# Two pieces of work for the output projection move from its first steps into the last unit of attention

## The chip, the cores and the metric

The kernel runs on one core of a Trainium2 chip. A core has five engines, each with its own instruction queue that is worked off strictly in order: PE (TensorE, matrix products), DVE (VectorE), ACT (ScalarE), POOL (GpSimd) and SP (SyncE, here only a queue that issues transfers). Engines wait for each other through semaphores. The metric is the time of one execution on the device in microseconds; lower is better. All times below are in microseconds unless ns stands there.

## What is computed

```
xn = layernorm(x)                                   # 2048 tokens, 448 features
q, k, v = xn @ wq, xn @ wk, xn @ wv                 # 16 heads of 28, 4 blocks of 512 tokens
for each block s:
    a_dot = softmax(causal(q_s k_s^T)) v_s          # local attention
    a_mem = phi(q_s) M / (phi(q_s) z + 1e-6)        # memory of the blocks before
    o_s   = g * a_mem + (1 - g) * a_dot ;  M, z += phi(k_s)^T v_s, sum phi(k_s)
out = x + o @ wo + (sigmoid(xn @ w_gate) * (xn @ w_up)) @ w_down
```

All data are 32-bit floats. Products go through PE in a 32-bit format that keeps fewer bits, so both factors are split into a high part and a low remainder, and a product of 448 terms becomes eleven matrix instructions (high by high, high by low, low by high, for three chunks of 128 features and one of 64; in the code this list is `TERMS`).

## The kernel before

The kernel has a front part, in which x is normalised and transposed into four tiles `xs[0..3]` (one for each block of 512 tokens: 128 partitions, chunks 0 to 3 the high part, 4 to 6 the low one), and q, k, v are made and stored. Then one long part is written out by hand, and that is where the change is. It weaves three streams, each a Python generator that issues instructions up to its next `yield`:

- `gated()`, the feed-forward branch: `pgu` products (L254) of `xs` with the gate and up weights, `sg` (tanh on ACT, L261; product on DVE, L271), `hh` split into high (ACT, L277) and low (DVE, L280), and the `pd` products (L180) that DVE adds to `acc` (L182). It works on two columns of 128 hidden features at a time, and for these on the blocks 0 to 3. The six last groups of `pd` are left over (`rest`): two for block 2, then four for block 3.
- `attention()`, sixteen units of four heads, each unit two pairs of heads. A table of ticks sets the order: a unit has 28 ticks, and `at(tick, rank, work)` puts a step in a tick's list, where lower ranks come first. A pair has scores (`st`, L638), maxima, a subtraction in three parts (DVE, L702) and exponentials in three parts (ACT, L706); the next unit's ticks hold the unit's end: `finish`, the product `pa` (L724) of the exponentials `w` with the values, and then `back`, `divide`, `turn`, `store`, which transpose the result on DVE (L730, L736), divide it, and add it to the memory part in DRAM (`od`, a transfer from POOL's queue).
- `project()`, the output projection. For each tile of 128 tokens (four to a block) there is a split, `split_tokens(b, t)`: ACT copies the high part of the attention result `sums` into `xs` (L802), and DVE subtracts it to get the low part (two instructions, L109 and L110). Two steps after a tile's split comes its product `po` of eleven instructions (L820) with the output weights `wo`. DVE adds it to `acc` (L827), and the tile is stored (L829). One of the groups in `rest` follows each of the first six `po`.

`sums[b]` is read back from `od[b]` by eight transfers of SP's queue (`load_sums`, L796); for block 0 the first is given out after the last scores of the last pair but one. The `xs` tile of a block is used again for `sums`, since the feed-forward branch has read it for the last time by then. The two halves of `wo` are split by ACT (L92) and DVE (L93) during the last hidden features.

The tile scheduler is switched off in this part. The order in each engine's queue is the order in which the Python code calls the instructions, and only the semaphores are added. A main loop at the end takes a step of `gated()` or `project()` in turn and lets `attention()` catch up to its share.

Of the kernel before, what the change touches and what calls it, by code (L numbers as in the profile page):

```python
# [11 lines left out]
AF = mybir.ActivationFunctionType  # L12
# [4 lines left out]
P = 128  # L17
# [21 lines left out]
TICKS = 28  # L39
# [3 lines left out]
SUBTRACT = ((22, 25, 26), (33, 34, 37))  # L43
EXPONENTS = ((25, 27, 31), (34, 36, 39))
BEHIND = (17, 18, 19, 24)
SUMS, END = 15, 25


# [20 lines left out]
def kernel(  # L69
# [11 lines left out]
    V, A, G, T = nc.vector, nc.scalar, nc.gpsimd, nc.tensor  # L81
# [6 lines left out]
    xs = [keep.tile([P, 7, L], F32R, name=f"xs{b}") for b in range(NB)]  # L88
# [18 lines left out]
    def transpose_low(p3, dst, t):  # L107
        tok = slice(t * P, (t + 1) * P)
        V.tensor_sub(dst[:, 4:7, tok], p3[:, 0:3], dst[:, 0:3, tok].bitcast(F32))  # L109
        V.tensor_sub(dst[64:, 3, tok], p3[64:, 3], dst[64:, 3, tok].bitcast(F32))  # L110
# [11 lines left out]
    def bank(name, tag):  # L122
        return ps.tile([P, L], F32, name=name, tag=tag, bufs=banks[tag])
# [177 lines left out]
    with tc.tile_pool(name="front", bufs=2) as sb, tc.manual_schedule(engines=FRONT):  # L301
# [227 lines left out]
        for b in range(NB):  # L529
# [24 lines left out]
            for k, c in enumerate((3, 4, 5, 6, 0, 1, 2) if last else range(7)):  # L554
# [34 lines left out]
                n = k - 1 if b == 0 else k + 1  # L589
# [152 lines left out]
    pairs = [Pair(n) for n in range(NB * H // 2)]  # L742
    units = [Unit(u, pairs[2 * u:2 * u + 2]) for u in range(NB * NG)]

    def attention():
        for n in range(2):
            pairs[n].load()
        units[0].load_values()
        yield
        plan = [[] for _ in range(n_att + 1)]  # L750

        def at(tick, rank, work, *args):
            plan[tick].append((rank, work, args))

        def following(n):
            if n < len(pairs):
                pairs[n].load()
            else:
                load_sums(n - len(pairs))

        for n, pair in enumerate(pairs):
            first = TICKS * (n // 2)
            ticks = [first + tick for tick in SCORES[n % 2]]
            for k, tick in enumerate(ticks):
                at(tick, 0, pair.score, k)
            at(ticks[-1], 2, following, n + 2)
            for k in range(3):
                at(first + MAXIMA[n % 2][k], 3, pair.maximum, k + 2)
                at(first + SUBTRACT[n % 2][k], 5, pair.subtract, k)
                at(first + EXPONENTS[n % 2][k], 1, pair.exponents, k)  # L770
            for k in range(4):
                at(first + JOINS[n % 2][k], 4, pair.join, k)
        for u, unit in enumerate(units):
            first = TICKS * (u + 1)
            at(first + SUMS, 1, unit.finish)
            if u + 1 < len(units):
                at(first + SUMS, 2, units[u + 1].load_values)
            for tick, work in zip(BEHIND, (unit.back, unit.divide, unit.turn, unit.store)):
                at(first + tick, 6, work)
        for work in plan:  # L780
            for _, run, args in sorted(work, key=lambda w: w[0]):
                run(*args)
            yield

    sums = {}

    def load_sums(b):

        if b < 2:
            sums[b] = sb.tile([P, HG, L], F32, name="sums", tag="qk2", bufs=2)  # L790
        else:
            sums[b] = sums[b - 2]
        o3 = od[b].rearrange("(h c) n -> h c n", c=32)
        for m in range(8):
            a, c = m % 2, 4 * min(m, 6)
            nc.sync.dma_start(sums[b][64 * a:64 * a + 64, m // 2, :], o3[:, c:c + 4, :])  # L796

    def project():

        def split_tokens(b, t):  # L800
            o3 = sums[b][:, :, t * P:(t + 1) * P]
            A.activation(xs[b][:, 0:4, t * P:(t + 1) * P], o3, AF.Copy)  # L802
            transpose_low(o3, xs[b], t)

        def out_weights(w):
            at = 2 * D * (w // 4) + D * (w % 2)
            return wo[w % 4 // 2][:, at:at + D]

        yield
        for n in range(NB * NT + 2):  # L810
            if n < NB * NT:
                b, t = divmod(n, NT)
                split_tokens(b, t)
                if t == NT - 1 and b + 2 < NB:
                    load_sums(b + 2)
            if n >= 2:
                b, t = divmod(n - 2, NT)
                po = bank("po", ("p", "gu")[n % 2])
                for m, (a, w) in enumerate(TERMS):
                    T.matmul(po[:, :D], xs[b][:, a, t * P:(t + 1) * P], out_weights(w),  # L820
                             start=m == 0, stop=m == len(TERMS) - 1)
                    if m in (3, 7):
                        yield
                halves = 2 if n == NB * NT + 1 else 1
                for i in range(halves):
                    part = slice(D // halves * i, D // halves * (i + 1))
                    V.tensor_add(acc[b][:, t, part], po[:, part], acc[b][:, t, part])  # L827
                    queue = nc.scalar if i else nc.sync
                    queue.dma_start(out[b * L + t * P:b * L + (t + 1) * P, part], acc[b][:, t, part])  # L829
                yield  # L830
                if rest:
                    yield from rest.pop(0)

    N_OUT = 1 + NB * NT * 3 + 12
    steps = attention()
    n_att = len(units) * TICKS + END
    done = 0
    with tc.manual_schedule(engines=MANUAL):
        next(steps)
        k = sum(FILLS) + 6  # L840
        for part in (ffn, project()):
            for _ in part:
                want = min(round(n_att * (k - LEAD) / (N_FFN + N_OUT - LEAD - TAIL)), n_att)
                k += 1
                while done < want:
                    next(steps)
                    done += 1
# [39 lines left out]
```

## Time and profile before

| | |
|---|---|
| median of 3 runs | 687.49 (686.54 to 687.96) |
| the profiled execution's own time | 686.53 |
| its span, first to last instruction | 684.8 |
| granted TensorE clock | 1.000 |
| PE busy | 678.9 |
| DVE busy | 570.8 |
| ACT busy | 338.6 |
| POOL busy | 141.6 |

The profile is of one execution. A line that names an engine, a source line and an operation gives the tiles as "written <- read", then shapes, and "x11" for eleven instructions in a row. PEld is the loading of weights into PE, beside PE itself. "SPq" and "ACTq" are an engine's queue at work on something that isn't counted as busy, such as a wait or a transfer that is issued. A bracket such as [0.67 <-DVE xs L109] says that the engine stood idle for 0.67 us before this work, and that DVE's work on `xs` in line 109 ended the wait. PE's instructions overlap: the duration of one is its way through the array, and the distance from start to start is what it costs in a stream.

### The profile page before, as it was taken

The numbers are of one execution on the slowest core, as the hardware profiler recorded it, in microseconds if no ns is written. First come the engines' busy times: TensorE is split into PE (matmuls) and PEld (weight loads), VectorE is DVE, ScalarE is ACT, GpSimd is POOL, SyncE is SP. The second block draws the span as 40 slices with busy tenths as digits, with TensorE's granted clock in tenths as the row PEclk, the third lists the DMA queues.
The fourth block names the chain that finished last, engine by engine and source line by source line (L and its number), as shares of the span: only waits on it lengthen the run. The fifth ranks groups of instructions, "written<-read, shape, count | busy, mean of one in ns | idle before, by whom it ended". The sixth has DMA issues, their size and how long they took to land.

```text
span 684.8 us, 10503 instructions
## 1 busy us (share of the span) xinstructions
PE 678.9 (99%) x3594; PEld 567.8 (83%) x3594; DVE 570.8 (83%) x995; ACT 338.6 (49%) x563; POOL 141.6 (21%) x349
## 2 busy tenths in 40 slices
PE   8999999999999999999999999999999999999998
PEld 7898878778878788887888878888787887888797
DVE  6765695766799899999999899899998998999754
ACT  5837555343364445645456455455544554544320
POOL 3500010101212232232212213132122231321000
PEclk9999999999999999999999999999999999999999
DMA  7446556696224331252324442324352332423352
GB/s 268 182 151 234 203 208 243 245 335 184 71 73 99 95 100 58 58 154 61 96 56 101 96 113 60 100 57 105 85 111 69 97 74 72 106 71 85 82 168 104
DMA packets 45940, 84.37 MB, mean 123 GB/s; under 512 B 6336, under 2 KB 20544, under 8 KB 45376
## 3 DMA queue, kind: packets, MB, share of 16 engines
q1 hardware_dynamic: 42736, 76.26, 37.0%
q0 software_dynamic: 3008, 7.34, 5.0%
q8 instruction: 28, 0.46, 0.3%
q14 instruction: 24, 0.20, 0.1%
q10 hardware_dynamic: 144, 0.11, 0.0%
HBM read 51.05 MB, written 32.64 MB: 122 GB/s over the span
## 4 chain that ended last, share of the span: by engine, by line
PE 89%; DVE 7%; issue 2%; POOL 1%; ACT 1%; DMA 0%; DVEq 0%; ACTq 0%; POOLq 0%
PE pgu L254 37%; PE pd L180 18%; PE pp L380 10%; PE st L638 5%; PE po L820 5%; PE pa L724 5%; PE pv L360 5%; PE pmm L408 2%; PE n L426 2%; DVE w L702 1%; DVE mx L660 1%; PE pt L102 1%; PE pk L400 1%; DVE acc L182 1%; DVE sg L271 0%
## 5 line engine op out<-in xcount | busy, mean ns | idle before, releaser
L254 PE MATMUL pgu<-xs,wgu 128*128 128x512 f32 x1232 | 302.6, 393 | 0.0
L254 PEld LDWEIGHTS pgu<-xs,wgu 128*128 128x128 f32 x1232 | 229.1, 188 | 46.2 <-issue 2.0
L180 PE MATMUL pd<-wdn,hh 128*128 128x448 f32 x672 | 155.3, 366 | 0.0
L180 PEld LDWEIGHTS pd<-wdn,hh 128*128 128x128 f32 x672 | 122.8, 188 | 11.5 <-issue 0.8
L653 POOL TENSOR_SCALAR_AFFINE_SELECT w<-w 128x256 f32<-128x256 f32 (+1 forms) x160 | 76.0, 478 | 231.2 <-ACT w L642 162.8
L706 ACT ACTIVATE w<-w 128x1024 f32<-128x1024 f32 (+1 forms) x96 | 87.9, 916 | 58.0 <-DVE w L702 58.0
L642 ACT ACTIVATE w<-st 128x512 f32<-128x512 f32 x128 | 75.7, 592 | 61.5 <-PE st L638 55.9
L702 DVE TENSOR_TENSOR w<-w,mb 128x1024 f32<-128x1024 f32 (+1 forms) x96 | 100.7, 1055 | 0.8
L660 DVE TRANSPOSE_TENSOR_REDUCE mx<-w 128x32 f32<-128x1024 f32 x64 | 79.0, 1234 | 6.6 <-POOL w L653 6.5
L380 PE MATMUL pp<-xs,wqk 128*128 128x512 f32 x308 | 77.7, 402 | 0.0
L182 DVE TENSOR_TENSOR acc<-pd,acc 128x448 f32<-128x448 f32 x112 | 67.6, 603 | 5.5 <-PE pd L180 5.5
L277 ACT ACTIVATE hh<-sg 128x512 fp32r<-128x512 f32 x56 | 35.4, 631 | 67.3 <-DVE sg L271 45.6
L380 PEld LDWEIGHTS pp<-xs,wqk 128*128 128x128 f32 x308 | 56.8, 188 | 13.4 <-issue 2.4
L638 PE MATMUL st<-qk 84*128 84x128 f32 (+3 forms) x256 | 62.0, 314 | 0.0
L261 ACT ACTIVATE sg<-pgu 128x512 f32<-128x512 f32 x56 | 33.2, 593 | 50.7 <-PE pgu L254 48.8
L638 PEld LDWEIGHTS st<-qk 84*128 84x128 f32 x256 | 47.9, 189 | 8.7 <-issue 1.4
L271 DVE SCALAR_TENSOR_TENSOR sg<-sg,pgu 128x512 f32<-128x512 f32 x56 | 37.8, 674 | 10.8 <-PE pgu L254 10.8
L387 DVE TENSOR_TENSOR qk<-pp,qk 128x512 fp32r<-128x512 f32 x28 | 19.3, 689 | 29.8 <-ACT e L385 23.7
L688 DVE STREAM_TRANSPOSE mb<-top 128x1024 f32<-128x1024 f32 x32 | 39.5, 1235 | 3.3 <-POOL top L685 3.2
L360 PE MATMUL pv<-wv,xs 128*128 128x448 f32 x176 | 39.6, 376 | 0.3 <-POOL wv L457 0.2
L280 DVE SCALAR_TENSOR_TENSOR hh<-sg,hh 128x512 fp32r<-128x512 f32 x56 | 38.2, 682 | 0.9 <-ACT hh L277 0.9
L724 PE MATMUL pa<-w,vv 128*32 128x128 f32 (+3 forms) x512 | 37.8, 436 | 0.0
(100 smaller groups left out, 638.5 us busy)
## 6 DMA issues: line engine op xcount, KB each, us to landing
qk<-qd SPq DMA_DIRECT2D x192, 112.0 KB
qd<-qk SPq DMA_DIRECT2D x28, 512.0 KB
raw<-in_w_ffn SPq DMA_DIRECT2D x14, 512.0 KB
vd<-vst SPq DMA_DIRECT2D x4, 1024.0 KB
vv<-vd SPq DMA_DIRECT2D x16, 256.0 KB
od<-w POOLq DMA_DIRECT2D x16, 256.0 KB, 4.2
sums<-od SPq DMA_DIRECT2D x32, 128.0 KB
out<-acc SPq DMA_DIRECT2D x15, 224.0 KB
```

Of the source, the lines that this page charges most:

```text
L180: T.matmul(pd[:, :D], l, r, start=n == 0, stop=n == len(mms) - 1)
L182: V.tensor_add(acc[b][:, t, :], pd[:, :D], acc[b][:, t, :])
L254: T.matmul(dst, wgu[f][:, w, side * P:(side + 1) * P], xs[b][:, a, :], start=n == 0, stop=n == len(TERMS) - 1)
L360: T.matmul(pv[:, :D], xs[b][:, a, t * P:(t + 1) * P], wv[w], start=n == 0, stop=n == len(TERMS) - 1)
L380: T.matmul(pp, wqk[c][:, w, :], xs[b][:, a, :], start=n == 0, stop=n == len(TERMS) - 1)
L638: T.matmul(st[:, at:at + L - kb * P], self.qk[:KS, 1, h, kb * P:(kb + 1) * P], self.qk[:KS, 0, h, kb * P:], start=True, stop=True)
L642: A.activation(w, st, AF.Copy)
L653: G.affine_select(d, d, pattern=pattern, base=0, channel_multiplier=-1, compare_op=ALU.is_ge, fill=MASK)
L660: V.tensor_reduce(self.mx[:, 32 * h:32 * h + 32], w3[:, h, :2 * L].rearrange("p (b n) -> p b n", n=32), axis=mybir.AxisListType.X, op=ALU. ...
L702: V.tensor_sub(w, w, m)
L706: A.activation(w, w, AF.Exp, scale=SCALE)
L724: T.matmul(pa[32 * j:32 * j + 32, kb * P:], self.vv[:, kb, 32 * j:32 * j + 32], self.pairs[j // 2].block(j % 2, kb), start=kb == 0, stop=k ...
```

## The change

The splits of the first two tiles (block 0, tiles 0 and 1) are given out at ticks 10 and 12 of the last unit's trailing ticks, with the highest rank, 7, so as the last thing in their tick. They fall out of the projection's loop, which begins its splits with the third tile. `split_tokens` moves up so that both streams can call it. With that, all line numbers rise, by 1 up to line 745 and by 4 to 8 below; the copy of the high part becomes L748, and DVE's two instructions become L110 and L111.

```diff
+EARLY_SPLITS = (10, 12)
 ...
+    def split_tokens(b, t):
+        o3 = sums[b][:, :, t * P:(t + 1) * P]
+        A.activation(xs[b][:, 0:4, t * P:(t + 1) * P], o3, AF.Copy)
+        transpose_low(o3, xs[b], t)
+
     def attention():
 ...
             for tick, work in zip(BEHIND, (unit.back, unit.divide, unit.turn, unit.store)):
                 at(first + tick, 6, work)
+        for t in range(2):
+            at(TICKS * len(units) + EARLY_SPLITS[t], 7, split_tokens, 0, t)
 ...
     def project():
-        def split_tokens(b, t):
 ...
                 b, t = divmod(n, NT)
-                split_tokens(b, t)
+                if n > 1:
+                    split_tokens(b, t)
```

On DVE, at the seam between attention and projection, the rows before are these. `xs_65` is the tile of block 0, `acc_71` the sum of block 2, and L730 is `back` of the last unit. The last two rows are the split of tile 0, and the same two stand behind them for tile 1 and for tile 2.

```order
L702 TENSOR_TENSOR w<-w,mb 128x2x2x128
L182 TENSOR_TENSOR acc_71<-pd,acc_71 128x448
L93 TENSOR_TENSOR wo<-raw,wo 128x896
L271 SCALAR_TENSOR_TENSOR sg<-sg,pgu 128x512
L182 TENSOR_TENSOR acc_71<-pd,acc_71 128x448
L280 SCALAR_TENSOR_TENSOR hh<-sg,hh 128x512
L730 STREAM_TRANSPOSE w<-pa 128x512
L109 TENSOR_TENSOR xs_65<-sums,xs_65 128x3x128
L110 TENSOR_TENSOR xs_65<-sums,xs_65 64x128
```

And on DVE now:

```order
L703 TENSOR_TENSOR w<-w,mb 128x2x2x128
L110 TENSOR_TENSOR xs_65<-sums,xs_65 128x3x128
L111 TENSOR_TENSOR xs_65<-sums,xs_65 64x128
L183 TENSOR_TENSOR acc_71<-pd,acc_71 128x448
L110 TENSOR_TENSOR xs_65<-sums,xs_65 128x3x128
L111 TENSOR_TENSOR xs_65<-sums,xs_65 64x128
L94 TENSOR_TENSOR wo<-raw,wo 128x896
L272 SCALAR_TENSOR_TENSOR sg<-sg,pgu 128x512
L183 TENSOR_TENSOR acc_71<-pd,acc_71 128x448
L281 SCALAR_TENSOR_TENSOR hh<-sg,hh 128x512
L731 STREAM_TRANSPOSE w<-pa 128x512
```

The pairs of tile 0 and tile 1 moved up, past `wo`, `sg`, `hh`, `back` and two additions to `acc`; the pair of tile 2 now stands right behind `back`.

On ACT, at the same seam, with the semaphores that each row waits for, before:

```order
L706 ACTIVATE w<-w 128x2x2x256 [waits DVE_49,Activation_49,Pool_49]
L706 ACTIVATE w<-w 128x2x2x128 [waits DVE_49,Pool_49]
L92 ACTIVATE wo<-raw 128x896 [waits DMAHW7_49]
L277 ACTIVATE hh<-sg 128x512 [waits DVE_49]
L802 ACTIVATE xs_65<-sums 128x4x128 [waits DMAHW4_49,DMAHW5_49,DMAHW3_49,DMAHW6_49,DMAHW2_49,DMAHW7_49,DMAHW1_49,DMAHW0_49]
L802 ACTIVATE xs_65<-sums 128x4x128 x3
```

And on ACT now:

```order
L707 ACTIVATE w<-w 128x2x2x256 [waits DVE_49,Activation_49,Pool_49]
L748 ACTIVATE xs_65<-sums 128x4x128 [waits DMAHW4_49,DMAHW5_49,DMAHW3_49,DMAHW6_49,DMAHW2_49,DMAHW7_49,DMAHW1_49,DMAHW0_49]
L707 ACTIVATE w<-w 128x2x2x128 [waits DVE_49,Pool_49]
L748 ACTIVATE xs_65<-sums 128x4x128
L93 ACTIVATE wo<-raw 128x896
L278 ACTIVATE hh<-sg 128x512 [waits DVE_49]
L748 ACTIVATE xs_65<-sums 128x4x128 x2
```

The first copy, with its wait for the eight transfers of `sums`, moved ahead of the last exponentials of attention, and the second stands right behind them. On PE, POOL and SP the order of the instructions is the same as before; what PE waits for changes.

More of the change, by code (lines that the diff above doesn't have):

```diff
@@ L798, in project @@
     def project():
-        def split_tokens(b, t):
-            o3 = sums[b][:, :, t * P:(t + 1) * P]
-            A.activation(xs[b][:, 0:4, t * P:(t + 1) * P], o3, AF.Copy)
-            transpose_low(o3, xs[b], t)
         def out_weights(w):
```

## The prediction

> **What bounds the kernel now.** I read the page's first part first: who is busy.
>
> ```profile
> span 684.8 us, 10503 instructions
> PE 678.9 (99%) x3594; PEld 567.8 (83%) x3594; DVE 570.8 (83%) x995; ACT 338.6 (49%) x563; POOL 141.6 (21%) x349
> PEclk9999999999999999999999999999999999999999
> ```
>
> PE is busy 678.9 of 684.8 us at the full granted clock. An edit that leaves PE's work as it is can only win PE's idle time, 5.9 us in all, and only the part of it that the moved work causes. So the next view is PE's waits from 600 us on (total, times, longest), and after it PE's instructions in order of time around the seam between attention and projection (start, duration, what, and in brackets the idle time before it).
>
> ```profile
> PE po L820 <- DVE xs L109: 0.7, 1, 0.7
> ```
>
> ```profile
> 634.19 1.38 PE L180 MATMUL pd<-wdn,hh 128*128 128x448 f32 x6
> 635.50 2.36 PE L724 MATMUL pa<-w,vv 128*32 128x512 f32 x32
> 637.79 0.68 PE L820 MATMUL po<-wo,xs 128*128 128x448 f32 x2
> 639.13 2.08 PE L820 MATMUL po<-wo,xs 128*128 128x448 f32 x9 [0.67 <-DVE xs L109]
> 641.05 1.36 PE L180 MATMUL pd<-wdn,hh 128*128 128x448 f32 x6
> 642.25 2.36 PE L820 MATMUL po<-wo,xs 128*128 128x448 f32 x11
> 644.45 1.36 PE L180 MATMUL pd<-wdn,hh 128*128 128x448 f32 x6
> ...
> 647.85 1.36 PE L180 MATMUL pd<-wdn,hh 128*128 128x448 f32 x6
> ...
> 659.25 22.16 PE L820 MATMUL po<-wo,xs 128*128 128x448 f32 x110
> ```
>
> In these last 85 us PE waits once. The first product of the projection starts when `pa` is done. Its first two instructions run, the third needs the low part of `xs`, and DVE hasn't written that yet. After 639.13 PE has no gap up to its last matrix instruction, so whatever is won at this place reaches the end, and nothing more can be won there. Behind PE's end stand only the last addition and the last transfer, which the change doesn't touch.
>
> Why is DVE late? Its own instructions in order of time:
>
> ```profile
> 632.32 0.69 DVE L702 TENSOR_TENSOR w<-w,mb 128x512 f32<-128x512 f32 x1
> 632.92 0.62 DVE L182 TENSOR_TENSOR acc<-pd,acc 128x448 f32<-128x448 f32 x1
> 634.60 1.09 DVE L93 TENSOR_TENSOR wo<-raw,wo 128x896 fp32r<-128x896 f32 x1 [1.06 <-ACT wo L92]
> 635.61 0.68 DVE L271 SCALAR_TENSOR_TENSOR sg<-sg,pgu 128x512 f32<-128x512 f32 x1
> 636.21 0.62 DVE L182 TENSOR_TENSOR acc<-pd,acc 128x448 f32<-128x448 f32 x1
> 636.99 0.69 DVE L280 SCALAR_TENSOR_TENSOR hh<-sg,hh 128x512 fp32r<-128x512 f32 x1 [0.16 <-ACT hh L277]
> 637.92 0.72 DVE L730 STREAM_TRANSPOSE w<-pa 128x512 f32<-128x512 f32 x1 [0.24 <-PE pa L724]
> 638.57 0.52 DVE L109 TENSOR_TENSOR xs<-sums,xs 128x384 fp32r<-128x384 f32 x1
> 639.11 0.29 DVE L110 TENSOR_TENSOR xs<-sums,xs 64x128 fp32r<-64x128 f32 x1
> 639.43 0.56 DVE L109 TENSOR_TENSOR xs<-sums,xs 128x384 fp32r<-128x384 f32 x1
> ```
>
> The split that PE needs (638.57) stands in the queue behind `back` (637.92), which itself has to wait for the end of `pa`. So the split can't begin before PE is through with `pa`, and PE wants it 0.4 us later. Meanwhile DVE was idle for 1.06 us at 633.5.
>
> **The removed wait.** The row says 0.67 us of idle, but in a stream PE pays from start to start. The disturbed product takes 641.05 - 637.79 = 3.26 us up to the next group, the next one 644.45 - 642.25 = 2.20 us. The wait therefore costs 3.26 - 2.20 = 1.06 us. The two ends are 0.67 (the idle row alone) and 1.06; I take 1.06, because it compares two starts of the same eleven instructions, and the instruction's way through the array stands in the idle row's place on both sides. A page of the Trainium skill puts the undisturbed product lower: "TensorE: Matmul & The Clock Gate", section "Back-to-back issue gap", gives a lone stream N/2.4 + 2.5 ns, for N = 448 some 189 ns, while the trace has 2.20 / 11 = 200 ns; by the page eleven would take 2.08 us and the gain would be 1.18 us, by the row 1.06, and the row decides.
>
> **What moves on ACT.** ACT's instructions in order of time, the copies' durations (least, median, most), and the chain of waits where the copies begin:
>
> ```profile
> 631.67 1.06 ACT L706 ACTIVATE w<-w 128x1024 f32<-128x1024 f32 x1
> 633.10 0.64 ACT L706 ACTIVATE w<-w 128x512 f32<-128x512 f32 x1 [0.37 <-DVE w L702]
> 633.64 0.94 ACT L92 ACTIVATE wo<-raw 128x896 fp32r<-128x896 f32 x1
> 636.33 0.63 ACT L277 ACTIVATE hh<-sg 128x512 fp32r<-128x512 f32 x1 [1.76 <-DVE sg L271]
> 636.87 4.26 ACT L802 ACTIVATE xs<-sums 128x512 fp32r<-128x512 f32 x8
> ```
>
> ```profile
> L802 ACT ACTIVATE xs<-sums x16: 612/614/633, 636.9 to 666.1; 128x512 fp32r<-128x512 f32 x16
> ```
>
> ```profile
> 636.39 0.04 ACTq L802
> ...
> 636.95 0.04 ACTq L802
> ```
>
> A copy takes 0.61 us, and in a row one starts every (4.26 - 0.61) / 7 = 0.52 us. The first now stands between the exponentials of 631.67 and of 633.10. It can start at about 632.65 and ends at 633.27. The last exponentials waited until 633.10 for DVE anyway, so they move by about 0.1 us, to 633.2, and end at 633.8. The copy also brings its wait for eight transfers to this place, and behind it stand those exponentials. If the transfers have landed, it is only the queue's steps: before, they ran from 636.39 to 636.95, beside the running `hh` copy (636.33 to 636.96), so they cost nothing, and now they run beside exponentials of 1.06 us. The upper bound, if nothing hid them, is 636.95 - 636.39 = 0.56 us more. PE enters `pa`, which needs these exponentials, at 635.50, 1.76 us after their old end of 633.74, so 0.1 and 0.66 both vanish. Have the transfers landed? SP's queue issued them from 608.28, and the DMA share (second last figure) falls to zero long before 632.6:
>
> ```profile
> 608.28 5.73 SPq L796 DMA_DIRECT2D sums<-od  x8
> ```
>
> ```profile
> 616.00:617.00 1.00, 1.00 (x6) 0.86 (x5) 1.00 (x2) 0.37 (x1) 0.82 (x2) 1.00 0.63 186
> 617.00:618.00 1.00, 1.00 (x6) 0.83 (x5) 1.00 (x3) 0.00 (x0) 0.00 (x0) 1.00 0.00 1
> ```
>
> That leaves some 15 us of slack. The second copy takes 633.7 to 634.35, and the copy of `wo` moves from 633.64 to about 634.3, ending at 635.2 in place of 634.58. On the path: 0.
>
> **What moves on DVE.** A split pair costs 639.43 - 638.57 = 0.86 us, two 1.72. The first starts with ACT's copy, at about 633.3, and ends at 634.15. The addition to `acc` (0.5 to the next start) follows, then the second pair from 634.65 to 635.5, and `wo` from 635.5 to 636.6 in place of 634.60 to 635.69. So 1.06 us of the 1.72 fall into the idle time that stood there, and what follows moves by about 0.9 us. Who waits for that?
> - PE's eighth `po` instruction is the first that needs the low part of the second half of `wo`: 637.79 + 7 x 0.20 = 639.2, against 636.6. Slack 2.6 us.
> - `sg` goes from 635.61 to about 636.5, and so ACT's `hh` to 637.2 and DVE's low `hh` to about 638.6 in place of 637.68. Only block 3's `pd` reads them, and its first group is the one at 647.85, the third of the six left over. Slack over 8 us.
> - The second addition to block 2's `acc` ends at about 637.7 in place of 636.83 and frees a PSUM bank that PE next wants for the group at 644.45, 1.06 us earlier now. Slack over 5 us.
> - `back` goes from 637.92 to about 638.5. But the two pairs behind it are gone, so the third tile's split starts at about 639.2 (before: after 640.3), while its product starts at about 644.6 (before 645.65). `divide`, `turn` and the store of the last unit come about 1 us earlier too.
>
> On the path: 0. SP's, POOL's and PE's queues keep their order, and no transfer is added. What hides the moved work is DVE's idle 1.06 us and the slack before `pa`; were that cover gone, each microsecond by which the last exponentials end after `pa` has come to them would be one on PE. What is late next in place of the removed wait: nothing within 2.6 us.
>
> **Sum.** 684.8 - 1.06 = 683.7 us of span. The profiled execution took 686.53, that is 1.73 around the span, and would take 685.5; the median of the runs, 687.49, lies 0.96 above it, so the forecast in its terms is 686.4 us, 0.15% less.
>
> **Rivals.**
> 1. *The wait stays under another name, wholly or in part.* The place is the same product, and the row that could take over is the split of `wo` on DVE, which is now behind both pairs. For it: everything moved stands ahead of it. Against: 2.6 us of slack. From an end past 639.2 on each microsecond is lost, and at 640.3 the gain is gone: 687.5 us. If only the idle row's 0.67 is won, 686.8. A change that does nothing, since the wait for the low part would only be seen as something else's, would end here too.
> 2. *Slower, by ACT's queue.* The wait for the transfers now stands ahead of the last exponentials. If the first copy could start only where it did before, at 636.87, for a reason that the rows don't show, the exponentials would run from 637.4 to 638.05, and PE, which needs them from the second batch of `pa`'s weights on (635.95, below), would lose 2.1 us in `pa`. Less the 1.06 that are won, that is 1.0 us more: 688.5. It decides from a copy that starts past 634.8 (635.95 less 0.52 and 0.64), and the loss outweighs the gain past 635.9. Against: the DMA share is zero from 617 on.
>
> ```profile
> 635.95 0.13 PEld L724 LDWEIGHTS pa<-w,vv 128*32 128x32 f32 x4 [0.30 <-issue]
> ```
>
> **How the numbers follow.** The forecast has 0.78, rival 1 0.14 and rival 2 0.08. About 0.2% (1.4 us) is what a measurement of this kernel can tell from no change: the runs before span 1.42 us themselves. The forecast's 686.4 lies on the near side of the bound at 686.1; with a scatter of some half a microsecond a good third of its chance falls beyond it, 0.30. Rival 1 is within the bound. Rival 2 reaches it on the slow side in two of three cases, 0.05. That gives faster 0.30, same 0.65, slower 0.05. The range: the lowest run less the whole gain, 686.54 - 1.06 = 685.5, and the highest run with no gain, 687.96; I take 685.4 to 688.0.
>
> **What would show it.** In the changed kernel's trace PE should go from `pa` through eleven `po` without a bracket, the next `pd` 2.2 us after the first `po`, near 640.0; DVE's split pairs should stand near 633.3 and 634.7, ahead of `wo`, and its idle 1.06 us should shrink to a few tenths; ACT's last exponentials should end before 634; PE's only waits left should be those of the start. The prediction is wrong if `pa` starts later than 635.5 or shows a bracket, or if a `po` waits for `wo`, or if the trace is as forecast and the span isn't shorter.

## The result, and the profile after

| | before | after |
|---|---|---|
| median of 18 runs each | 686.98 | 685.74 |
| lowest to highest | 686.53 to 687.96 | 685.43 to 687.24 |
| ratio, 95% interval | 1 | 0.9983 (0.9976 to 0.9990) |
| span of the profiled execution | 684.8 | 684.2 |

The changed kernel is faster by 1.24 us, or 0.18%; the interval reaches from 0.7 to 1.6 us. The forecast was 686.4 within 685.4 to 688.0.

The page's head and PE's waits over the whole execution (total, times, longest) of the changed kernel:

```profile
span 684.2 us, 10501 instructions
PE 678.0 (99%) x3594; PEld 566.7 (83%) x3594; DVE 570.1 (83%) x995; ACT 338.5 (49%) x563; POOL 141.6 (21%) x349
```

```profile
PE warm L468 <- POOL ident masks.py:199: 1.5, 1, 1.5
PE pt L103 <- DVE xn L346: 0.7, 1, 0.7
PE pv L361 <- DVE xs L110: 0.3, 1, 0.3
```

The wait of `po` is gone. All three waits that are left belong to the first 12 us. PE at the seam, in order of time:

```profile
635.82 2.36 PE L725 MATMUL pa<-w,vv 128*32 128x512 f32 x32
638.11 2.48 PE L824 MATMUL po<-wo,xs 128*128 128x448 f32 x11
640.42 1.36 PE L181 MATMUL pd<-wdn,hh 128*128 128x448 f32 x6
641.62 2.36 PE L824 MATMUL po<-wo,xs 128*128 128x448 f32 x11
643.82 1.36 PE L181 MATMUL pd<-wdn,hh 128*128 128x448 f32 x6
```

The eleven instructions of the first product now stand in one row, and the next group starts 640.42 - 638.11 = 2.31 us after them, where it was 3.26. So the seam gave 0.95 us. The second product takes 2.20, as before. DVE and ACT there:

```profile
632.64 0.68 DVE L703 TENSOR_TENSOR w<-w,mb 128x512 f32<-128x512 f32 x1
633.59 0.56 DVE L110 TENSOR_TENSOR xs<-sums,xs 128x384 fp32r<-128x384 f32 x1 [0.27 <-ACT xs L748]
634.18 0.29 DVE L111 TENSOR_TENSOR xs<-sums,xs 64x128 fp32r<-64x128 f32 x1
634.48 0.62 DVE L183 TENSOR_TENSOR acc<-pd,acc 128x448 f32<-128x448 f32 x1
635.02 0.55 DVE L110 TENSOR_TENSOR xs<-sums,xs 128x384 fp32r<-128x384 f32 x1
635.59 0.29 DVE L111 TENSOR_TENSOR xs<-sums,xs 64x128 fp32r<-64x128 f32 x1
635.91 1.09 DVE L94 TENSOR_TENSOR wo<-raw,wo 128x896 fp32r<-128x896 f32 x1
...
638.90 0.71 DVE L731 STREAM_TRANSPOSE w<-pa 128x512 f32<-128x512 f32 x1
```

```profile
631.99 1.05 ACT L707 ACTIVATE w<-w 128x1024 f32<-128x1024 f32 x1
632.94 0.62 ACT L748 ACTIVATE xs<-sums 128x512 fp32r<-128x512 f32 x1
633.46 0.62 ACT L707 ACTIVATE w<-w 128x512 f32<-128x512 f32 x1
633.98 0.61 ACT L748 ACTIVATE xs<-sums 128x512 fp32r<-128x512 f32 x1
```

DVE's idle time of 1.06 us ahead of `wo` has become 0.27 us ahead of the first split. On ACT the first copy starts 0.95 us after the exponentials ahead of it, one instruction's distance: the eight waits for the transfers are not to be seen. The last exponentials end at 634.08, 1.74 us ahead of `pa`.

The spans differ by 0.6 us and not by 0.95, since `pa` starts 0.32 us later than before. That has nothing to do with the seam. In the front part, which is the same in both kernels, PE came to the first product with `wqk` later by 0.42 us (before, then after):

```profile
19.70 7.69 PE L380 MATMUL pp<-xs,wqk 128*128 128x512 f32 x33
```

```profile
20.12 7.64 PE L381 MATMUL pp<-xs,wqk 128*128 128x512 f32 x33
```

By the last `pgu` ahead of the seam it has become 632.00 - 631.67 = 0.33 us, and from there to `pa` it is 3.82 us where it was 3.83: nothing of the shift arises at the seam. From the start of `pa` to the end of the span it is 684.8 - 635.50 = 49.3 us before and 684.2 - 635.82 = 48.4 after.

### The profile page after: what moved, and what is told of

Read it like the earlier page. It is cut to its first block, busy times and chain, and to the rows that moved or that the text cites. A ratio compares the mean times of both kernels' runs of the same rounds, so it can differ in the third digit from the quotient of the medians.

```text
span 684.2 us, 10501 instructions
## 1 busy us (share of the span) xinstructions
PE 678.0 (99%) x3594; PEld 566.7 (83%) x3594; DVE 570.1 (83%) x995; ACT 338.5 (49%) x563; POOL 141.6 (21%) x349
## 4 chain that ended last, share of the span: by engine, by line
PE 97%; DMA 1%; DVE 1%; SPq 0%; ACT 0%; issue 0%; DVEq 0%
PE pgu L255 41%; PE pd L181 20%; PE pp L381 10%; PE st L639 6%; PE pa L725 5%; PE po L824 5%; PE pv L361 5%; PE pmm L409 2%; PE n L427 2%; DMA acc<-in_x 1%; PE pt L103 1%; PE pk L401 1%; DVE stats L320 0%; DVE xs L110 0%; DVE xn L346 0%
## 5 line engine op out<-in xcount | busy, mean ns | idle before, releaser
L262 ACT ACTIVATE sg<-pgu 128x512 f32<-128x512 f32 x56 | 33.2, 592 | 50.8 <-PE pgu L255 48.9
```

## Experiments

The theory is that of the prediction: PE waited for the low part of tile 0 alone, and this was late because in DVE's queue it stood behind `back`, which waits for `pa`. Rival A is that ACT's copies had to get out of the way; rival B, that most of the difference is a shift of the whole program; rival 1 of the prediction, that `wo` is late next; rival 2, that the wait for the transfers comes out at PE. The column "before, beside it" is the kernel before, measured together with the kernel of that row; the last column is taken from the traces.

| kernel | median | before, beside it | ratio (95%) | first `po` to the next group | `pa` to the end of the span |
|---|---|---|---|---|---|
| before | | | | 3.26 | 49.3 |
| changed | 685.74 | 686.98 | 0.9983 (0.9976 to 0.9990) | 2.31 | 48.4 |
| `back` later | 685.77 | 686.74 | 0.9987 (0.9978 to 0.9996) | 2.32 | 48.3 |
| tile 0 alone | 685.83 | 686.74 | 0.9984 (0.9976 to 0.9993) | 2.32 | 48.3 |
| tile 1 alone | 686.79 | 686.74 | 1.0002 (0.9993 to 1.0011) | 3.19, and 0.33 ahead of it | 49.6 |
| four tiles | 685.72 | 686.74 | 0.9984 (0.9975 to 0.9992) | 2.32 | 48.3 |
| ticks 2 and 4 | 685.66 | 686.76 | 0.9986 (0.9976 to 0.9995) | 2.31 | 48.4 |
| ticks -10 and -8 | 687.58 | 686.76 | 1.0008 (0.9999 to 1.0017) | 2.31 | 48.3 |

### Only `back` moves

```diff
 # the kernel before
-            for tick, work in zip(BEHIND, (unit.back, unit.divide, unit.turn, unit.store)):
+            behind = BEHIND if u + 1 < len(units) else (18, 18, 19, 24)
+            for tick, work in zip(behind, (unit.back, unit.divide, unit.turn, unit.store)):
```

> The kernel before, with one instruction moved: the last unit's `back` on DVE stands behind the three split pairs of block 0, not ahead of them. Nothing moves on ACT. Theory (the gain comes from DVE's queue, where the split that PE needs stood behind `back`, which waits for `pa`): the first split starts when the low `hh` is done, about 637.7 and not 638.6, so PE's third `po` waits at most 0.1 us; the first product takes 2.3 us and not 3.26; about 0.9 us faster than before, so a ratio near 0.9987. Rival A (the gain comes from ACT's copies being out of the way early): the product still takes 3.2 us, no change. Rival B (the difference of 1.2 us is mostly a shift of the whole program that has nothing to do with the seam): no change here either.

DVE and PE of this kernel around the seam, in order of time:

```profile
637.56 0.69 DVE L280 SCALAR_TENSOR_TENSOR hh<-sg,hh 128x512 fp32r<-128x512 f32 x1 [0.16 <-ACT hh L277]
638.17 0.55 DVE L109 TENSOR_TENSOR xs<-sums,xs 128x384 fp32r<-128x384 f32 x1
...
640.89 0.72 DVE L730 STREAM_TRANSPOSE w<-pa 128x512 f32<-128x512 f32 x1
```

```profile
638.36 2.48 PE L821 MATMUL po<-wo,xs 128*128 128x448 f32 x11
640.68 1.36 PE L180 MATMUL pd<-wdn,hh 128*128 128x448 f32 x6
```

One DVE instruction moved by six places (three pairs) gives the whole gain: 2.32 us for the product, ratio 0.9987. ACT's queue is that of the kernel before, so rival A falls. Rival B falls with "tile 1 alone" below: there more of the program is changed than here, and nothing is gained. The first row of the split begins 0.2 us ahead of the first `po` and ends, at 638.72, 0.04 us ahead of the third `po`, which wants it at 638.36 + 2 x 0.20 = 638.76: just in time, where the change itself has 4 us to spare.

### One tile alone

```diff
 # the changed kernel, tile 0 alone; for tile 1: range(1, 2) and n != 1
-        for t in range(2):
+        for t in range(1):
             at(TICKS * len(units) + EARLY_SPLITS[t], 7, split_tokens, 0, t)
 ...
-                if n > 1:
+                if n > 0:
                     split_tokens(b, t)
```

> The changed kernel with the split of tile 0 alone given out early; tile 1 is split at the head of the projection, as before the change. Theory: PE waited for tile 0 alone, so the whole gain is there: first product 2.3 us, no wait of PE, the time of the changed kernel within 0.2 us, a ratio near 0.998 to the kernel before. Rival A (both copies have to be out of ACT's way): half of the gain, ratio 0.999. Tile 1's split would end about 640.4, its product starts at 641.6, so it isn't late.

> The changed kernel with the split of tile 1 alone given out early, tile 0 at the head of the projection. Theory: tile 0's split still stands behind `back`, and the low `hh` ahead of it starts some 0.6 us later, because the moved pair (0.86 us) stands in the queue and only part of it falls into the idle time: PE's third `po` starts about 0.3 us later than in the kernel before, the first product takes 3.5 us, the kernel is 0.3 us slower than before or the same (ratio 1.000 to 1.0005). Rival A (moving ACT's copies early is what helps): a gain of half a microsecond.

PE with tile 0 alone:

```profile
638.00 2.48 PE L824 MATMUL po<-wo,xs 128*128 128x448 f32 x11
640.32 1.36 PE L181 MATMUL pd<-wdn,hh 128*128 128x448 f32 x6
```

PE with tile 1 alone:

```profile
635.49 2.36 PE L725 MATMUL pa<-w,vv 128*32 128x512 f32 x32
638.11 0.67 PE L824 MATMUL po<-wo,xs 128*128 128x448 f32 x2 [0.26 <-ACT xs L748]
639.38 2.08 PE L824 MATMUL po<-wo,xs 128*128 128x448 f32 x9 [0.60 <-DVE xs L110]
641.30 1.36 PE L181 MATMUL pd<-wdn,hh 128*128 128x448 f32 x6
```

ACT's copies of this kernel up to 640 us, of which the first is that of tile 0:

```profile
637.45 2.70 ACT L748 ACTIVATE xs<-sums 128x512 fp32r<-128x512 f32 x5
```

Tile 0 alone has the whole gain, tile 1 alone has none, and its trace is 0.3 us longer behind `pa`, as expected to a tenth; the times can't tell that from nothing (1.0002). One thing was not expected: with tile 1 alone the first `po` itself starts late, 638.11 where `pa`'s 2.29 us would have it at 637.78. ACT's copy of tile 0 ended only at 637.45 + 0.61 = 638.06, since it stands behind the `hh` copy, and that moved with `sg` (from 636.33 to 636.91). The sum, 641.30 - 637.78 = 3.52, is what was expected, but in two waits. So the second half of the change, tile 1's early split, is worth nothing that these runs can tell, and costs nothing.

### Twice the moved work

```diff
 # the changed kernel
-EARLY_SPLITS = (10, 12)
+EARLY_SPLITS = (10, 12, 12, 12)
 ...
-        for t in range(2):
+        for t in range(4):
 ...
-                if n > 1:
+                if n > 3:
```

> The changed kernel with all four splits of block 0 given out early, tiles 2 and 3 right behind tile 1. It doubles the work that stands ahead of `wo`, `sg` and `hh` on DVE, by 1.72 us. Theory (there are 2.6 us of slack behind the moved work): `wo` is ready at about 638.7 and PE's eighth `po` comes to it at about 639.5, so PE waits for nothing and the time is that of the changed kernel within 0.2 us, ratio near 0.998. Rival 1 of the prediction (the wait goes over to `wo`): a wait of PE at the eighth `po`, and a time 0.5 us or more above that of the changed kernel.

`wo` on DVE and the first product on PE:

```profile
637.79 1.09 DVE L94 TENSOR_TENSOR wo<-raw,wo 128x896 fp32r<-128x896 f32 x1
```

```profile
638.24 2.48 PE L824 MATMUL po<-wo,xs 128*128 128x448 f32 x11
640.56 1.36 PE L181 MATMUL pd<-wdn,hh 128*128 128x448 f32 x6
```

`wo` is ready at 638.88, and the eighth `po` comes to it at 638.24 + 7 x 0.20 = 639.64. No wait, and the time of the changed kernel. Rival 1 has no ground here even with 3.4 us of moved work in place of 1.7; 0.76 us of slack are left.

### Earlier, where DVE has no idle time, and where the transfers haven't landed

```diff
 # the changed kernel
-EARLY_SPLITS = (10, 12)
+EARLY_SPLITS = (2, 4)        # and, in a kernel of its own, (-10, -8)
```

> The changed kernel with the two splits 8 ticks earlier (ticks 2 and 4). On DVE they stand ahead of the transpose that makes `mb`, so ahead of the subtractions and exponentials of the last pair, where DVE has no idle time but 0.37 us. Theory (the slack ahead of `pa` is 1.76 us, and the two pairs cost 1.72 less that 0.37): the last exponentials end about 1.3 us later, near 635.4 (by the times of the profile before), just ahead of `pa`; PE waits for at most a few tenths, and the gain stays: ratio near 0.9985 to the kernel before. Rival (DVE is the bound here, and what is put ahead of the exponentials comes out at PE in full): `pa` 1.3 us later, the gain gone, ratio 1.0003.

> The changed kernel with the two splits 20 ticks earlier (ticks -10 and -8), three ticks after the first transfers of `sums` are given out: the cover of the transfers is gone. Theory: ACT's copy waits until the transfers have landed, about 617 in the profile before, where its place in the queue comes up near 612.7; tanh and the copies of scores behind it come some 3 us late, DVE's split pair holds DVE for nearly as long, and since DVE has about 1.4 us of idle time from there to the seam, one to three microseconds reach PE: 686.7 to 688.7, so the gain is lost and more. Rival (the wait is absorbed, since ACT is busy for half of the time): the time of the changed kernel.

Ticks 2 and 4, ACT's last exponentials and PE:

```profile
635.15 0.63 ACT L707 ACTIVATE w<-w 128x512 f32<-128x512 f32 x1 [0.38 <-DVE w L703]
```

```profile
631.79 2.68 PE L255 MATMUL pgu<-xs,wgu 128*128 128x512 f32 x11
...
635.61 2.36 PE L725 MATMUL pa<-w,vv 128*32 128x512 f32 x32
637.90 2.48 PE L824 MATMUL po<-wo,xs 128*128 128x448 f32 x11
640.21 1.36 PE L181 MATMUL pd<-wdn,hh 128*128 128x448 f32 x6
```

The last `pgu` of the kernel before:

```profile
631.67 2.68 PE L254 MATMUL pgu<-xs,wgu 128*128 128x512 f32 x11
```

Measured from the last `pgu`, the exponentials start 635.15 - 631.79 = 3.36 us behind it, where it was 633.10 - 631.67 = 1.43. So they are 1.9 us later and not 1.3: the idle 0.37 us was not filled, because DVE's first pair stands behind the instruction that waits there. That accounts for 1.72 us, the whole of the two pairs; the last 0.2 us stay unexplained. The exponentials end at 635.78, 0.17 us after `pa` has begun, and PE still waits for nothing: in the code only the part of `pa` from the second batch of weights on reads them, and that batch is loaded at 636.07. The gain stays, ratio 0.9986. From the first pair to the last exponentials DVE is busy without a gap, and still isn't the bound.

Ticks -10 and -8, ACT, DVE and PE:

```profile
616.78 0.63 ACT L748 ACTIVATE xs<-sums 128x512 fp32r<-128x512 f32 x1 [3.89 <-DMA sums<-od]
...
624.05 0.63 ACT L278 ACTIVATE hh<-sg 128x512 fp32r<-128x512 f32 x1 [4.16 <-DVE sg L272]
...
626.96 0.59 ACT L262 ACTIVATE sg<-pgu 128x512 f32<-128x512 f32 x1
```

```profile
617.45 0.56 DVE L110 TENSOR_TENSOR xs<-sums,xs 128x384 fp32r<-128x384 f32 x1 [2.35 <-DMA vv<-vd]
```

```profile
624.38 2.68 PE L255 MATMUL pgu<-xs,wgu 128*128 128x512 f32 x11
627.60 1.47 PE L181 MATMUL pd<-wdn,hh 128*128 128x448 f32 x6 [0.54 <-ACT sg L262]
...
632.71 2.70 PE L255 MATMUL pgu<-xs,wgu 128*128 128x512 f32 x11
636.18 1.48 PE L181 MATMUL pd<-wdn,hh 128*128 128x448 f32 x6 [0.78 <-ACT sg L262]
637.60 2.36 PE L725 MATMUL pa<-w,vv 128*32 128x512 f32 x32
```

Here the wait that rival 2 of the prediction fears is made to happen. ACT stands still for 3.9 us and DVE for 2.35. (The bracket of DVE's row names the transfer of `vv`; but the row reads ACT's copy, and starts 0.04 us after that has ended, at 617.41.) The kernel takes 687.58, 1.8 us more than the changed one and 1.9 more than ticks 2 and 4 beside it, within what was expected. The first product is as short as in the changed kernel; the loss comes ahead of it, and not where I had placed it: not at `pa`, but at two `pd` groups that wait for tanh (L262) to be done with a PSUM bank. Tanh is late, at 626.96 where the kernel before has it at 623.27, because it stands in ACT's queue behind instructions that wait for DVE, and DVE is late.

## Why the prediction was right

- *The bound.* That PE is the bound, that its one wait in the last 85 us is at the third `po`, and that whatever is won there reaches the end: the wait is gone and the time behind `pa` fell from 49.3 to 48.4 us. That only PE's idle time can be won, as the prediction has it, does not quite hold: 0.28 of the 0.95 us had been counted as busy (last section).
- *The removed wait.* Forecast 1.06 us, measured 0.95 in the trace. The term was too large by 0.11: it compared the first product with the second, 2.20 us. But the first one takes 2.31 or 2.32 us in all six kernels in which PE doesn't wait in it. The second follows a `pd`, and its weight loads begin 0.2 us ahead of its first instruction; the first follows `pa`, and its loads begin with it (changed kernel: 641.42 for 641.62, and 638.11 for both). Whether that is the cause was not tried. The estimate from the spacing of a lone product in the Trainium skill ("TensorE: Matmul & The Clock Gate", "Back-to-back issue gap"), some 189 ns where the trace has 200, was 1.18 us, further off than the row.
- *The moved work.* The cost of 0 held, on ACT and on DVE. `wo` ended at 637.0 (forecast 636.6), the last exponentials at 634.08 (633.8), the first pair started at 633.59 (633.3). All three are later by 0.3 to 0.4 us, of which the front part has 0.3. The slack was there: `wo` was ready 2.5 us ahead of the eighth `po` (forecast 2.6), and doubled work (four tiles) and work put ahead of the exponentials (ticks 2 and 4) both left the gain whole.
- *The sum.* 0.15% was forecast and 0.18% measured, with 0.10 to 0.24 in the interval. The seam in the trace is 0.14%. The surplus is within the scatter; the lowest runs differ by 1.10 us (686.53 and 685.43). In us the forecast was 0.66 too high, 686.4 against 685.74, mostly because it started from a median of three runs, 687.49; from that of 18, 686.98, the same sum gives 685.9. The prediction also held that less than 0.2% can't be told from no change. With 18 runs of each kernel 0.18% can: the interval stays clear of 1.
- *The signs.* One of the signs that were to show it wrong did appear: `pa` started at 635.82, later than 635.5. It was a badly chosen sign, since a shift of the whole program by 0.3 us sets it off; measured from the last `pgu`, `pa` came when it did before. So do the last exponentials, which end 2.08 us behind the start of that `pgu` (before 2.07), though at 634.08 and not before 634.
- *The rivals.* The first did not come true, and with twice the work it still doesn't. The second needs a copy that is given out before its transfers land. In the change they had landed 15 us earlier. With ticks -10 and -8 that wait was there and cost 1.8 us, but by tanh and `pd`, not by the exponentials and `pa` as the rival has it.

## What to carry to other kernels

When one engine is the bound and waits once, look at what stands ahead of the late instruction in the queue of the engine that makes it, and not only at how long that takes. Here the late split stood behind an instruction that waits for PE itself, and moving either of the two by a few places took the same 0.9 us out of PE's path. Before moving work up, find the end of its inputs' transfers: the same move made 20 ticks earlier cost at least what it had won (ratio to the kernel before 1.0008, 0.9999 to 1.0017).

## What was not expected of the hardware

- An idle row of PE was less than the wait cost, in all three cases here. The row said 0.67 us, and removing it won 0.95. The rest stood in the row ahead of it: two `po` are shown with 0.68 us there, while two in a stream cost 2 x 0.20 = 0.40, and 0.67 + 0.28 = 0.95. With ticks -10 and -8 the rows of 0.54 and 0.78 us stand for 627.60 - 624.38 - 2.52 = 0.70 and 636.18 - 632.71 - 2.52 = 0.95 (2.52 us from a `pgu` to the `pd` behind it without a wait, 634.19 - 631.67 before).
- The start of `pa` lies between 635.49 and 636.07 in the first five kernels' traces and in that of before, with the same work of PE ahead of it. Only part of it comes from the front part: with `back` later the first product with `wqk` is late by 0.08 us and `pa` by 0.57, and 0.5 of that arises between 503 and 554 us, where PE waits once for ACT (0.24 us at 541.91). This scatter is over half of the whole effect, so one pair of spans would have misjudged it; the seam's own distance, 2.31 or 2.32, hardly varies at all.
